# Seed products, clamps and K's skip term computed by GpSimd, x's first two splits in another order, and the last bank copied by ScalarE alone

## The chip, the cores and the metric

The kernel runs on one core of a Trainium2 chip. The metric is the device time of one execution in microseconds (us). Engines are named as the profile has them: PE is TensorE's matmul, PEld its weight load, DVE is VectorE, ACT is ScalarE, POOL is GpSimd, SP is SyncE, which here only issues DMAs.

## The reference

Two independent heads are computed and concatenated along the last axis. All inputs are fp32.

```python
# head A: FNet mixing, x is [1, 2048, 512]
a = jnp.einsum("bsd,ed->bse", x, dft_hid_re)
b = jnp.einsum("bsd,ed->bse", x, dft_hid_im)
y = jnp.einsum("ts,bse->bte", dft_seq_re, a) - jnp.einsum("ts,bse->bte", dft_seq_im, b)
...
# head B: S4D convolution, 512 channels, 128 states, length 2048
P = jnp.exp((A * dt[:, None])[:, :, None] * pos[None, None, :])
K = 2.0 * jnp.einsum("dn,dnl->dl", C, P).real
y = jnp.fft.irfft(jnp.fft.rfft(u_t, L2) * jnp.fft.rfft(K, L2)[None], L2)[:, :, :L]
y = y.transpose(0, 2, 1) + u * D_skip
```

## The kernel before, in words

**Head A** (class `Fnet`) is two stages of matmuls in split precision. Every fp32 operand is split into a high part, rounded to the type that PE multiplies fast, and a low part, the remainder; one product is then three matmuls of 128x128 by 128x512 (L371): high by high, high by low, low by high. `split` (L222) writes the high part on ScalarE (L226) and the low part on VectorE (L230). Stage "s" multiplies x, kept in SBUF as 16 tiles, with 8 blocks of the sequence matrices; stage "p" multiplies the transformed weights with the results. There are 128 streamed tiles in the first stage and 32 in the second, and the 28 of the first that `SOFTS` lists are split by DMA: POOL issues a load of the tile (L320), ScalarE writes its negative (L323), and POOL issues a second load that adds the source (L325). The four split tiles in flight come free when PE has used them. `evacuate` (L381) copies a finished bank on ScalarE (L396) and stores it; the very last bank is copied in halves, the right one by VectorE (L389) and the left one by ScalarE (L391), with one DMA each from SP and ScalarE.

**Head B** (class `Ssm`) builds the kernel K from two tables of complex powers per channel. The 512 channels go in 16 chunks of 32. For each chunk `seed_args` (L644) makes the arguments of the seeds on ScalarE, takes the phase's distance from its nearest whole number on VectorE (L662), clamps it to plus or minus a half (L664, the clamp, 352 elements a partition), and takes absolute value, exponential and sines on ScalarE (L666 to L674). `seeds` (L678) multiplies cosine and sine with the decay (L683, the product, 704 elements a partition, written with a stride of two) and ScalarE copies the result with either sign (L688). `tables1` and `tables2` double the tables with products and sums on VectorE (L613, L622, L636, L642) and squares on ScalarE (L629). `taps` multiplies the tables on PE (L809), ScalarE copies the taps `ks` to SBUF (L819), and `stage1_k` (L827) adds the skip term to one position (L832, 16 elements a partition) and runs the first half of K's transform on PE (L858). The spectra of u and K are then formed, multiplied (L1021 to L1057) and transformed back (L1064, L1136, L1158), through DRAM.

**What sets the order.** The program holds generators that yield the engine they want and a cost; `Plan` runs them against estimated clocks and thereby writes one fixed order for each engine, each of which runs it in order. A `yield "dve", ...` decides when the instruction behind it is emitted, whichever engine that instruction is for. So PE's order is fixed too: an L809 or L1064 that waits for VectorE holds up the L371 matmuls behind it.

Of the kernel before, what the change touches and what calls it, by code (L numbers as in the profile page):

```python
# [8 lines left out]
F32 = mybir.dt.float32  # L9
F32R = mybir.dt.float32r  # L10
I32 = mybir.dt.int32
AF = mybir.ActivationFunctionType
OP = mybir.AluOpType
# [3 lines left out]
SEQ, DM, NS = 2048, 512, 128  # L17
# [170 lines left out]
def act(cols):  # L188
    return 0.09 + cols * 0.00085


def dve(cols, rate=1.0):
    return (66 + cols / rate) / 960
# [6 lines left out]
class Fnet:  # L200
# [4 lines left out]
    def __init__(self, tc, ctx, plan, x, wT, sT, out):  # L205
        self.tc, self.nc, self.plan = tc, tc.nc, plan
        self.xin, self.wT, self.sT, self.out = x, wT, sT, out
        self.psum = ctx.enter_context(tc.tile_pool(name="a_psum", bufs=4, space=PSUM))
        self.pool = ctx.enter_context(tc.tile_pool(name="a", bufs=1))
        self.acc, self.raws, self.ss, self.ys = Sem(4), Sem(RAWS), Sem(DEPTH), Sem(STAGED)  # L210
        dram = ctx.enter_context(tc.tile_pool(name="a_dram", bufs=1, space=DRAM))
        self.p = {(t, c, d): dram.tile([128, DM], F32, name=f"p{t}_{c}_{d}")
                  for t in range(4) for c in range(2) for d in range(4)}
        self.p_ev = {k: Event() for k in self.p}
        self.x, self.w = [None] * 16, [None] * 8
        self.x_ev, self.w_ev, self.x_free = ([Event() for _ in range(n)] for n in (16, 8, 16))
        self.groups = [("s", t, c) for t in range(4) for c in range(2)] + [("p", t, None) for t in range(4)]
        self.items = {g: [(*g, k) for k in range(16 if g[0] == "s" else 8)] for g in self.groups}
        self.split_ahead, self.x0_ev, self.hi_ev = 0, Event(), Event()
        self.m, self.m_ev = {}, {i: Event() for g in self.groups for i in self.items[g]}  # L220

    def split(self, hi, lo, src):  # L222
        def urgency():
            return 3 if self.split_ahead >= AHEAD else 0
        yield "act", act(512), urgency
        self.nc.scalar.activation(hi, src, AF.Copy)  # L226
        if self.hi_ev.time is None:
            self.plan.set(self.hi_ev)
        yield "dve", dve(512), urgency
        self.nc.vector.tensor_tensor(lo, src, hi.bitcast(F32), op=OP.subtract)  # L230

    def start(self, buffers):
# [40 lines left out]
    def load_x1(self, b, raw, n):  # L273
        cols = slice(0 if n else 128, DM)
        yield "dma", load(256)
        self.nc.sync.dma_start(raw[:, cols], self.xin[n, :, cols])
        if n:
            self.x[n] = self.still(n)
        else:
            yield self.hi_ev  # L280
        yield from self.split(*(a[:, cols] for a in self.x[n]), raw[:, cols])
        self.plan.set(self.x_ev[n])
        self.x_left -= 1
        if not self.x_left:
            self.plan.put(b.uks)
# [95 lines left out]
    def evacuate(self, g, d, ps):  # L381
        yield self.ys
        y = self.pool.tile([128, DM], F32, name="y", bufs=STAGED)
        if g == self.groups[-1] and d == 3:
            out = self.out[128 * d:128 * d + 128, 512 * g[1]:512 * g[1] + 512]
            yield self.ys
            y2 = self.pool.tile([128, DM], F32, name="y", bufs=STAGED)
            yield "dve", dve(256)
            self.nc.vector.tensor_copy(y2[:, 256:], ps[:, 256:])  # L389
            yield "act", act(256)  # L390
            self.nc.scalar.activation(y[:, :256], ps[:, :256], AF.Copy)  # L391
            self.nc.sync.dma_start(out[:, 256:], y2[:, 256:])
            self.nc.scalar.dma_start(out[:, :256], y[:, :256])
            return
        yield "act", act(512)
        self.nc.scalar.activation(y, ps, AF.Copy, scale=-1.0 if g[2] == 1 else 1.0)  # L396
        self.plan.put(self.acc)
        if g != self.groups[-1]:
            yield "dma", load(256)
        kind, t, c = g  # L400
        if kind == "s":
            self.nc.sync.dma_start(self.p[t, c, d], y)
            self.plan.set(self.p_ev[t, c, d])
        else:
            self.nc.sync.dma_start(self.out[128 * d:128 * d + 128, 512 * t:512 * t + 512], y)
        self.plan.put(self.ys)
# [29 lines left out]
class Ssm:  # L436
# [207 lines left out]
    def seed_args(self, ck, box, ev):  # L644
# [9 lines left out]
        n = 11 * CHUNK  # L654
# [6 lines left out]
        yield "dve", dve(n)  # L661
        v.scalar_tensor_tensor(r, k, RND, r, op0=OP.subtract, op1=OP.subtract)  # L662
        yield "dve", dve(n, 2)
        v.tensor_scalar(r, r, 0.5, -0.5, op0=OP.min, op1=OP.max)  # L664
        yield "act", act(n)
        a.activation(k, r, AF.Abs)  # L666
        yield "act", act(n) + 1.3
# [10 lines left out]
    def seeds(self, ck, s):  # L678
# [1 line left out]
        yield self.css  # L680
        cs = self.tab.tile([128, 2, 11, CHUNK, 2], F32, name="cs", bufs=2)
        yield "dve", dve(22 * CHUNK)
        self.nc.vector.tensor_tensor(cs[:, :, :, :, 0], s[:, 1:3], s[:, 0:1].to_broadcast([128, 2, 11, CHUNK]),  # L683
                                     op=OP.mult)
        self.plan.put(self.res)
        for n, sign in enumerate((1.0, -1.0)):
# [140 lines left out]
    def stage1_k(self, ks, n, ev):  # L827
# [1 line left out]
        nc = self.nc  # L829
        yield ev  # L830
        yield "dve", dve(16)
        nc.vector.tensor_tensor(ks[:, 0], self.dskip[:, 16 * n:16 * n + 16], ks[:, 0], op=OP.add)  # L832
        yield self.const_ev
        got = yield from self.banks(2)
        xs = []
# [415 lines left out]
```

## Time and profile before

| | |
|---|---|
| median of 3 runs | 578.18 us (577.84 to 579.45) |
| profiled execution | 578.43 us, of which its span, first to last instruction, 576.6 us |
| granted TensorE clock | 0.998 |
| PE, PEld busy | 567.8 us (98%), 432.5 us (75%) |
| DVE, ACT, POOL busy | 523.1 us (91%), 371.1 us (64%), 40.2 us (7%) |
| chain that ended last | PE 53%, DVE 34%, issue 7% |

A row of a group reads: line, engine, operation, output from inputs, shapes, count, then busy us and the mean ns of one, then the idle time of the engine ahead of it and who ended it. A row of the timeline or of the chain begins with the start in us and the length in us. A row of a stage begins with the stretch and its length. A busy PE is the modelled length of its matmuls, which overlap, so a short wait can hide beneath one.

### The profile page before, as it was taken

How to read it: one execution, taken by the hardware profiler on the slowest of the kernel's cores; microseconds unless marked ns; L12 is line 12 of the kernel's file. 1: busy time of each engine (PE TensorE's matmuls, PEld its weight loads, DVE VectorE, ACT ScalarE, POOL GpSimd, SP SyncE). 2: the span in 40 equal slices, each digit the busy share in tenths (PEclk: the TensorE clock that was granted, in tenths of full speed). 3: DMA queues.
4: the chain of work that ended last, by engine and by line, in shares of the span. 5: the costliest groups of instructions: out<-in, count | busy, mean ns of one | idle time of the engine just before them, and what ended most of it. 6: DMA issues, size and time to landing. Idle time of an engine off the chain costs nothing.

```text
span 576.6 us, 15666 instructions
## 1 busy us (share of the span) xinstructions
PE 567.8 (98%) x6278; PEld 432.5 (75%) x6278; DVE 523.1 (91%) x928; ACT 371.1 (64%) x728; POOL 40.2 (7%) x60
## 2 busy tenths in 40 slices
PE   8999999999999999999999999999999999999997
PEld 6877777788777777778787777777787778776785
DVE  6999999999999999999999999999998999547732
ACT  4779766673777495858669576754588845355623
POOL 0000101000110000100100100001100000000000
PEclk9999999999999999999999999999999999999999
DMA  8999999997469767867796888559998996599994
GB/s 250 326 386 251 285 282 278 278 281 185 123 160 231 196 175 235 202 165 217 194 251 197 220 202 252 142 155 259 288 295 227 237 311 207 129 278 265 256 254 147
DMA packets 147976, 133.70 MB, mean 232 GB/s; under 512 B 47296, under 2 KB 107328, under 8 KB 147648
## 3 DMA queue, kind: packets, MB, share of 16 engines
q1 hardware_dynamic: 138976, 115.54, 66.7%
q0 software_dynamic: 8064, 14.68, 13.1%
q10 hardware_dynamic: 864, 2.49, 1.9%
q8 instruction: 49, 0.80, 0.6%
q14 instruction: 23, 0.19, 0.1%
HBM read 89.95 MB, written 42.73 MB: 230 GB/s over the span
## 4 chain that ended last, share of the span: by engine, by line
PE 53%; DVE 34%; issue 7%; DMA 3%; ACT 3%; SPq 0%; DVEq 0%; ACTq 0%
PE acc L371 41%; DVE prod L613 11%; DVE t L622 6%; DVE lo L230 5%; PE f L1037 4%; PE f L1064 3%; PE f L809 3%; DVE t L642 2%; DMA out_yb<-zl 1%; DVE cs L683 1%; DVE z L1021 1%; DVE uk L1023 1%; PE f L858 1%; DMA zl<-zs 1%; DVE zl L925 1%
## 5 line engine op out<-in xcount | busy, mean ns | idle before, releaser
L371 PE MATMUL acc<-hi,x_hi 128*128 128x512 f32 x640 | 257.9, 403 | 0.5 <-ACT x_hi L226 0.4
L371 PE MATMUL acc<-lo,x_hi 128*128 128x512 f32 x640 | 250.1, 391 | 0.0
L371 PE MATMUL acc<-hi,x_lo 128*128 128x512 f32 x640 | 249.6, 390 | 0.0
L613 DVE TENSOR_TENSOR prod<-t,cs 128x1024 f32<-128x1024 f32 (+4 forms) x192 | 163.1, 868 | 1.7 <-ACT t L731 0.6
L371 PEld LDWEIGHTS acc<-hi,x_hi 128*128 128x128 f32 x640 | 120.0, 187 | 49.7 <-issue 23.8
L371 PEld LDWEIGHTS acc<-hi,x_lo 128*128 128x128 f32 x640 | 120.2, 188 | 26.5 <-DVE x_lo L230 0.5
L371 PEld LDWEIGHTS acc<-lo,x_hi 128*128 128x128 f32 x640 | 120.2, 188 | 23.3 <-DVE lo L230 0.4
L226 ACT ACTIVATE hi<-raw 128x512 fp32r<-128x512 f32 x132 | 82.6, 628 | 68.2 <-PE acc L371 53.2
L230 DVE TENSOR_TENSOR lo<-raw,hi 128x512 fp32r<-128x512 f32 x132 | 90.1, 685 | 23.8 <-ACT hi L226 23.1
L622 DVE TENSOR_TENSOR t<-prod 128x512 f32<-128x512 f32 (+4 forms) x192 | 94.1, 511 | 1.0
L629 ACT ACTIVATE square<-t 128x256 f32<-128x256 f32 (+1 forms) x64 | 36.7, 573 | 29.3 <-DVE t L622 26.8
L325 POOL DMA_DIRECT2D lo<-in_sT x28 | 24.3, 867 | 214.1 <-DVE t L622 40.0
L1016 ACT ACTIVATE uk<-f 128x1024 f32<-128x1024 f32 x32 | 31.1, 1017 | 10.8 <-PE f L1037 7.8
L809 PEld LDWEIGHTS f<-t,t 128*32 128x32 f32 x2048 | 29.5, 110 | 7.4 <-issue 5.2
L396 ACT ACTIVATE y<-acc 128x512 f32<-128x512 f32 x47 | 27.8, 595 | 10.5 <-PE acc L371 10.3
L809 PE MATMUL f<-t,t 128*32 128x64 f32 x2048 | 32.4, 220 | 1.3 <-issue 0.8
L320 POOL DMA_DIRECT2D hi<-in_sT x28 | 16.1, 575 | 189.2 <-PE acc L371 148.6
L1079 ACT ACTIVATE z<-f 128x512 f32<-128x512 f32 x32 | 17.8, 592 | 13.1 <-PE f L1064 12.0
L1021 DVE TENSOR_TENSOR z<-uk 128x512 f32<-128x512 f32 x32 | 21.9, 684 | 4.4 <-ACT uk L1016 2.9
L642 DVE TENSOR_TENSOR t<-square 128x128 f32<-128x128 f32 (+1 forms) x64 | 24.7, 386 | 0.0
L1037 PE MATMUL f<-xt,w 64*32 64x256 f32 x768 | 23.5, 379 | 0.0
L1023 DVE TENSOR_TENSOR uk<-uk 128x512 f32<-128x512 f32 x32 | 22.1, 691 | 0.9
(101 smaller groups left out, 502.9 us busy)
## 6 DMA issues: line engine op xcount, KB each, us to landing
raw<-in_sT SPq DMA_DIRECT2D x99, 256.0 KB, 5.2
p<-y SPq DMA_DIRECT2D x32, 256.0 KB, 3.5
xk<-xk_sb SPq DMA_DIRECT2D x32, 256.0 KB, 5.2
zs<-z SPq DMA_DIRECT2D x32, 256.0 KB, 3.9
raw<-p SPq DMA_DIRECT2D x32, 256.0 KB, 4.3
hi<-in_sT POOLq DMA_DIRECT2D x28, 256.0 KB, 4.6
lo<-in_sT POOLq DMA_DIRECT2D x28, 256.0 KB, 4.7
xt<-xu SPq DMA_DIRECT2D x24, 256.0 KB, 4.4
```

The source lines that it names most:

```text
L226: self.nc.scalar.activation(hi, src, AF.Copy)
L230: self.nc.vector.tensor_tensor(lo, src, hi.bitcast(F32), op=OP.subtract)
L371: nc.tensor.matmul(acc[d], l[:, cols], r, start=k == 0 and n == 0, stop=k == len(items) - 1 and n == 2)
L396: self.nc.scalar.activation(y, ps, AF.Copy, scale=-1.0 if g[2] == 1 else 1.0)
L613: self.nc.vector.tensor_tensor(p.rearrange("p k d c m -> p k (d c) m"), src.rearrange("p d c l -> p (d c) l")[:, None, :, rows].to_broadca ...
L622: self.nc.vector.tensor_tensor(dst[:, :, :, rows], p[:, 0], p[:, 1, :, ::-1], op=OP.add)
L629: self.nc.scalar.activation(sq, t[:, :, :, m // 2:m], AF.Square)
L642: self.nc.vector.tensor_tensor(t[:, :, 0, m:2 * m:2], box[0][:, :, 0], box[0][:, :, 1], op=OP.subtract)
L809: nc.tensor.matmul(ps[32 * j:32 * j + 32, i], t1[:, d, c], t2[:, d, c], start=c == 0, stop=c == 1, tile_position=(0, 32 * j))
L1016: a.activation(uk[:, r].rearrange("p g c n d -> p g (c n d)"), p, AF.Copy)
L1023: v.tensor_tensor(t[:, r], t[:, r], u[:, r, :, ::-1], op=OP.mult)
L1037: nc.tensor.matmul(got[r][1][32 * xx:32 * xx + 32, g, 256 * c:256 * c + 256], self.w2[rows, 2 * q + r, xx, 32 * c:32 * c + 32], xt[rows].r ...
```

## The change

Five edits. `split` takes the tiles of x's items 0 and 1 in the order in which its two steps come to run (`first`, `turns`), so that the rest of tile 0 is split ahead of tile 1 on ScalarE and on VectorE. The last bank is copied whole by ScalarE, and both DMAs read that copy. The clamp, the product and the skip term are instructions of GpSimd; the lines that yield a slot of VectorE for them stay as they were.

```diff
+        self.first, self.turns = {}, {"hi": [0, 1], "lo": [0, 1]}
...
-    def split(self, hi, lo, src):
+    def split(self, *tiles, n=None):
...
         yield "act", act(512), urgency
+        hi, _, src = tiles if n is None or n > 1 else self.first[self.turns["hi"].pop(0)]
         self.nc.scalar.activation(hi, src, AF.Copy)
...
         yield "dve", dve(512), urgency
+        hi, lo, src = tiles if n is None or n > 1 else self.first[self.turns["lo"].pop(0)]
         self.nc.vector.tensor_tensor(lo, src, hi.bitcast(F32), op=OP.subtract)
...
-        else:
+        tiles = (*(a[:, cols] for a in self.x[n]), raw[:, cols])
+        if n < 2:
+            self.first[n] = tiles
+        if not n:
             yield self.hi_ev
-        yield from self.split(*(a[:, cols] for a in self.x[n]), raw[:, cols])
+        yield from self.split(*tiles, n=n)
...
-            yield self.ys
-            y2 = self.pool.tile([128, DM], F32, name="y", bufs=STAGED)
-            yield "dve", dve(256)
-            self.nc.vector.tensor_copy(y2[:, 256:], ps[:, 256:])
-            yield "act", act(256)
-            self.nc.scalar.activation(y[:, :256], ps[:, :256], AF.Copy)
-            self.nc.sync.dma_start(out[:, 256:], y2[:, 256:])
+            yield "act", act(512)
+            self.nc.scalar.activation(y, ps, AF.Copy)
+            self.nc.sync.dma_start(out[:, 256:], y[:, 256:])
             self.nc.scalar.dma_start(out[:, :256], y[:, :256])
...
-        v.tensor_scalar(r, r, 0.5, -0.5, op0=OP.min, op1=OP.max)
+        self.nc.gpsimd.tensor_scalar(r, r, 0.5, -0.5, op0=OP.min, op1=OP.max)
...
-        self.nc.vector.tensor_tensor(cs[:, :, :, :, 0], s[:, 1:3], s[:, 0:1].to_broadcast([128, 2, 11, CHUNK]),
+        self.nc.gpsimd.tensor_tensor(cs[:, :, :, :, 0], s[:, 1:3], s[:, 0:1].to_broadcast([128, 2, 11, CHUNK]),
...
-        nc.vector.tensor_tensor(ks[:, 0], self.dskip[:, 16 * n:16 * n + 16], ks[:, 0], op=OP.add)
+        nc.gpsimd.tensor_tensor(ks[:, 0], self.dskip[:, 16 * n:16 * n + 16], ks[:, 0], op=OP.add)
```

Line numbers move by 3 to 7: L226, L230 and L371 become L229, L234 and L378, L664, L683 and L832 become L667, L686 and L835, and POOL's DMAs L320 and L325 become L327 and L332.

The first place is ScalarE at the start of the program, where `x_hi_140` is the rest of x's tile 0 and `x_hi_150` is tile 1. Before:

```order
L335 DMA raw<-in_sT 128x512
L226 ACT_TABLE_LOAD
L226 ACTIVATE hi<-raw 128x512
L226 ACTIVATE x_hi_150<-uk 128x512
L226 ACTIVATE x_hi_140<-uk 128x384
L226 ACTIVATE hi<-raw 128x512
```

And with the change:

```order
L342 DMA raw<-in_sT 128x512
L229 ACT_TABLE_LOAD
L229 ACTIVATE hi<-raw 128x512
L229 ACTIVATE x_hi_140<-uk 128x384
L229 ACTIVATE x_hi_150<-uk 128x512
L229 ACTIVATE hi<-raw 128x512
```

The two splits of x have changed places, and nothing else here; VectorE's low parts of the two tiles change places in the same way.

The second place is VectorE near the end of the fourth chunk's first table, `t_1803`, where the second skip term (`ks`) and the sixth chunk's product (`cs<-seed`) stood; `prod` and `prod_2062` are products for the tables, `lo` is the low part of a streamed tile. Before:

```order
L613 TENSOR_TENSOR prod<-t_1803,cs 128x1024
L230 TENSOR_TENSOR lo<-raw,hi 128x512
L622 TENSOR_TENSOR t_1803<-prod 128x32x16
L230 TENSOR_TENSOR lo<-raw,hi 128x512
L832 TENSOR_TENSOR ks<-dskip,ks 128x16
L683 TENSOR_TENSOR cs<-seed 128x704
L613 TENSOR_TENSOR prod_2062<-t_124,cs 128x128
L613 TENSOR_TENSOR prod<-t_1803,cs 128x1024
```

And with the change:

```order
L616 TENSOR_TENSOR prod<-t_1803,cs 128x1024
L234 TENSOR_TENSOR lo<-raw,hi 128x512
L625 TENSOR_TENSOR t_1803<-prod 128x32x16
L234 TENSOR_TENSOR lo<-raw,hi 128x512
L616 TENSOR_TENSOR prod_2062<-t_124,cs 128x128
L616 TENSOR_TENSOR prod<-t_1803,cs 128x1024
```

The skip term and the product are gone from VectorE, and what stood behind them follows at once; all else on VectorE keeps its order, and PE's order is the same from end to end.

The third place is POOL at about the same point; `hi` and `lo` are the tiles that POOL loads, and `seed_1821`, `ks_1476` and `cs_2051` belong to the sixth clamp, the second skip term and the sixth product. Before, POOL's rows there are DMAs alone:

```order
L325 DMA lo_1748<-in_sT 128x512
L320 DMA hi_1856<-in_sT 128x512
L325 DMA lo_1857<-in_sT 128x512
L320 DMA hi_2045<-in_sT 128x512
L325 DMA lo_2046<-in_sT 128x512
L320 DMA hi_2194<-in_sT 128x512
```

And with the change:

```order
L332 DMA lo_1748<-in_sT 128x512
L327 DMA hi_1856<-in_sT 128x512
L667 TENSOR_SCALAR seed_1821<-seed_1821 128x352
L332 DMA lo_1857<-in_sT 128x512
L835 TENSOR_TENSOR ks_1476<-dskip_112,ks_1476 128x16
L686 TENSOR_TENSOR cs_2051<-seed_1821 128x704
L327 DMA hi_2045<-in_sT 128x512
L332 DMA lo_2046<-in_sT 128x512
```

POOL's clamps, skip terms and products stand between the two loads of one tile or between two tiles, each behind whatever DMA comes ahead of it. One more row comes first of all on POOL, `L667 ISA`, ahead of the first clamp.

## The prediction

> **What bounds the kernel now.** I read the busy shares first, then the engines by stage, then the chain of waits, and last the rows of the moved instructions. The first line of the page has two full engines:
>
> ```profile
> PE 567.8 (98%) x6278; PEld 432.5 (75%) x6278; DVE 523.1 (91%) x928; ACT 371.1 (64%) x728; POOL 40.2 (7%) x60
> ```
>
> The busy time by stage (length, then PE, PEld, DVE, ACT, POOL) says where each of the two has room:
>
> ```profile
> 0.00:14.40 14.40, 12.28 (x44) 8.75 (x44) 10.02 (x25) 6.91 (x11) 0.20 (x4) 1.00 0.80 250
> 41.00:210.00 169.00, 167.51 (x1572) 128.55 (x1570) 167.34 (x298) 115.34 (x235) 17.77 (x25) 1.00 0.83 233
> 248.00:330.00 82.00, 81.95 (x1069) 64.05 (x1067) 81.17 (x143) 56.85 (x118) 7.95 (x12) 1.00 0.78 209
> 330.00:457.00 127.00, 125.91 (x1555) 95.86 (x1554) 123.84 (x224) 90.95 (x182) 10.52 (x15) 1.00 0.83 226
> 562.00:576.60 14.60, 10.61 (x164) 7.86 (x162) 4.18 (x7) 4.35 (x8) 0.00 (x0) 0.93 0.46 145
> ```
>
> PE idles 2.1 us in the first stage and 4.0 in the last. In the three stages between that are shown it idles 1.49 + 0.05 + 1.09 = 2.6 us. DVE has little more room: 1.66 us from 41 to 210, 0.83 from 248 to 330, and 3.16 from 330 to 457. The chain of waits, in order of time, tells which of the two leads:
>
> ```profile
> 41.20 0.69 DVE z L927
> ...
> 210.00 1.20 PE f L1064 x32
> ...
> 247.89 0.18 DVE lo L230
> ...
> 330.32 1.12 PE f L858 x32
> ```
>
> It runs mainly along DVE from 41 to 210 and from 248 to 330, and along PE from 210 to 248 and from 330 on. In the two DVE stretches a microsecond more on DVE is about a microsecond more at the end, since PE takes its work in a fixed order and its work is not shortened. A microsecond less on DVE gives something only while PE has a stall left to lose.
>
> **The DVE work that goes.** These three groups leave DVE (busy us and mean ns behind the first bar):
>
> ```profile
> L683 DVE TENSOR_TENSOR cs<-seed 128x704 f32<-128x704 f32 x16 | 14.2, 885 | 0.0
> L664 DVE TENSOR_SCALAR seed<-seed 128x352 f32<-128x352 f32 x16 | 5.3, 334 | 0.0
> L832 DVE TENSOR_TENSOR ks<-dskip,ks 128x16 f32<-128x16 f32 x8 | 1.3, 168 | 0.1
> ```
>
> Neighbours on DVE overlap a little, so the chain has what one really occupies:
>
> ```profile
> 59.04 0.25 DVE seed L664
> ...
> 77.92 0.80 DVE cs L683
> ```
>
> That is 0.80 us for a product and 0.25 for a clamp (a skip term is no more than the 0.17 of its row, and I leave it out). In the two DVE stretches of the chain lie so many (count, first and last start; products and clamps in 41 to 210, then in 248 to 330):
>
> ```profile
> L683 DVE TENSOR_TENSOR cs<-seed x6: 880/883/886, 54.6 to 185.9; 128x704 f32<-128x704 f32 x6
> L664 DVE TENSOR_SCALAR seed<-seed x7: 332/334/336, 43.9 to 205.9; 128x352 f32<-128x352 f32 x7
> ```
> ```profile
> L683 DVE TENSOR_TENSOR cs<-seed x3: 883/884/884, 270.7 to 318.7; 128x704 f32<-128x704 f32 x3
> L664 DVE TENSOR_SCALAR seed<-seed x3: 331/332/334, 261.6 to 310.1; 128x352 f32<-128x352 f32 x3
> ```
>
> So 9 products and 10 clamps count: 9 x 0.80 + 10 x 0.25 = 9.7 us of DVE time off the stretches that lead. Those elsewhere lie beside PE work that leads, and I cost them at nothing either way: after 330 DVE's 3.16 us of idle time is their cover.
>
> **What the same work costs on GpSimd.** No row has POOL computing; its rows are DMA issues and four memsets. The nearest rows are DVE's own (0.885 and 0.334 us) and ScalarE's:
>
> ```profile
> L1016 ACT ACTIVATE uk<-f 128x1024 f32<-128x1024 f32 x32 | 31.1, 1017 | 10.8 <-PE f L1037 7.8
> L1079 ACT ACTIVATE z<-f 128x512 f32<-128x512 f32 x32 | 17.8, 592 | 13.1 <-PE f L1064 12.0
> L666 ACT ACTIVATE seed<-seed 128x352 f32<-128x352 f32 x16 | 8.0, 497 | 10.8 <-DVE seed L664 10.7
> ```
>
> Below, DVE's own 0.885 and 0.334; above, the two inputs of a product read one after the other at DVE's price, 2 x 0.885 = 1.77, and 2 x 0.334 = 0.67 for a clamp. Between them lies ScalarE's rate: (1017 - 592) / 512 = 0.83 ns an element, so 2 x 704 elements read in turn are 0.592 + (1408 - 512) x 0.00083 = 1.34 us, and a clamp is 0.50 as in L666. I take 1.34 and 0.50, as the middle of either pair (estimates).
>
> **What DVE does meanwhile.** No row shows POOL reading tiles beside DVE, so this is bounded too: DVE goes on (POOL's time costs it nothing) or stands still for all of it. I take the second. Almost every DVE group in those stretches (L613, L622, L230, L642) reads two SBUF operands, as the products on GpSimd would, and I see nothing that serves both at once without cost; that is a choice, not a reading. The Trainium skill speaks for it: SBUF — State Buffer, "Who interferes with whom", says that a DVE instruction with two SBUF inputs contends with a GpSimd instruction that reads SBUF, and that the second to issue waits for the whole of the first; no run here shows it yet. The skill's GPSIMD Engine Reference, "Elementwise — side-by-side cycle accounting", has about 2.6 cycles an element for two inputs, which at its 1.2 GHz would be 1.53 us for a product, an estimate; with 0.50 for a clamp the sum below would have 9.1 instead of 7.4.
>
> With DVE standing still the net is +1.34 - 0.80 = +0.54 for a product and +0.50 - 0.25 = +0.25 for a clamp: 9 x 0.54 + 10 x 0.25 = **+7.4 us**. DVE's idle 1.66 + 0.83 us in the two stretches can lie beneath some of it; I take off 1.0.
>
> **The waits.** ScalarE's absolute value (L666) waits for the clamp and its copies (L688) for the product, as before. Behind them in ScalarE's order stand the splits (L226) for PE. POOL starts a clamp as soon as L662 is done, and need not pass the DVE instructions that stood between; a product waits on POOL for the DMAs ahead of it. The worst place (POOL, then ScalarE):
>
> ```profile
> 376.16 0.86 POOL L325 DMA_DIRECT2D lo<-in_sT  x1 [6.19 <-DVE t L622]
> ```
> ```profile
> 377.17 0.98 ACT L688 ACTIVATE cs<-cs 128x352 f32<-128x352 f32 x2
> ```
>
> There the DMA ends at 377.02 and the product at 377.02 + 1.34 = 378.36, so L688 is 1.2 us late, in the stretch where PE leads. I cost the waits at nothing: ScalarE is 64% busy. The price if that cover is gone is 1.2 us a place. The skip term is waited for by PE itself (L858), 0.6 us in one place; on POOL it can be 0.1 to 0.5 longer or as much earlier, and I take zero. DMAs queued behind POOL's new work are issued up to 1.84 us later; they had waited for buffers anyway. A new ISA row stands ahead of POOL's first clamp; its cover is the 24 us until the first clamp's input is there:
>
> ```profile
> 24.36 0.52 DVE L662 SCALAR_TENSOR_TENSOR seed<-seed 128x352 f32<-128x352 f32 x1
> ```
>
> **The start.** ScalarE now converts the rest of x's first tile before the second tile, and DVE likewise:
>
> ```profile
> 5.13 1.04 ACT L226 ACTIVATE x_hi<-uk 128x512 fp32r<-128x512 f32 x2 [0.57 <-DMA uk<-in_x]
> ```
> ```profile
> 5.34 0.50 PE L371 MATMUL acc<-lo,x_hi 128*128 128x512 f32 x1
> 6.23 0.51 PE L371 MATMUL acc<-hi,x_hi 128*128 128x512 f32 x1 [0.39 <-ACT x_hi L226]
> ...
> 7.35 0.40 PE L371 MATMUL acc<-hi,x_hi 128*128 128x512 f32 x1
> 7.58 0.39 PE L371 MATMUL acc<-lo,x_hi 128*128 128x512 f32 x1
> ```
>
> Fed matmuls start 0.23 us apart (7.35 to 7.58). From 5.34 to 7.35 are four steps in 2.01 us, which fed are 0.92: at most 1.1 us goes. But DVE leads from 41 us on and has no less to do before, so part of the head start is waited away: between 0 and 1.1, I take 0.5.
>
> **The end.** The last bank was copied by DVE and then by ScalarE, and the last DMA left at 573.57:
>
> ```profile
> 572.65 0.42 DVE L389 COPY y<-acc 128x256 f32<-128x256 f32 x1 [6.79 <-DMA out_yb<-zl]
> ...
> 573.57 0.36 ACTq L393 DMA_DIRECT2D out_ya<-y  x1
> ```
>
> Now one copy of 512 columns at 0.59 (as L1079) from 572.65 ends at 573.24, and both DMAs leave about 573.28: 0.3 us sooner.
>
> **The sum.** The profiled execution took 578.43 us, of which its span is 576.6; the median of the runs is 578.18, so I take 0.25 off. 578.43 + 7.4 - 1.0 - 0.5 - 0.3 - 0.25 = **583.8 us**. Its own range has the cheapest POOL with DVE standing, 9 x 0.085 + 10 x 0.084 - 1.8 = about -0.2, hence 578.0, and the dearest, 9 x 0.97 + 10 x 0.42 = 12.9 without idle time taken off, hence 578.18 + 12.9 - 0.3 = 590.8.
>
> **The rivals.** First, and on the other side: **DVE goes on beside POOL**. Then 9.7 us leave the leading stretches, and PE's stalls are the limit. They are the 2.6 us above, and what the modelled ends hide; the longest wait of the weight loads for DVE in 41 to 330 is
>
> ```profile
> PEld f L1064 <- DVE uk L1057: 1.4, 3, 0.6
> ```
>
> so 1.4 us in three waits. Both together are 4.0 us, and other weight loads that waited for DVE or ScalarE, once each, can add a little; I take 5 us of stalls as gone, and 1.0 at the start since DVE no longer leads: 578.18 - 5 - 1.0 - 0.3 = **571.9 us**. It decides where POOL's reads cost DVE less than the 1.05 us that a product and a clamp leave free. For it speaks that the 132 rows of one DVE form differ by 0.02 us at most, though POOL issued 56 DMAs in the same time:
>
> ```profile
> L230 DVE TENSOR_TENSOR lo<-raw,hi x132: 674/684/694, 4.6 to 559.8; 128x512 fp32r<-128x512 f32 x132
> ```
>
> Against it, that a DMA issue from POOL reads a tensor in HBM and no tile, so it is weak evidence for an instruction that reads tiles.
>
> Second: **the two cancel**, POOL nearly as quick as DVE, or DVE half stopped: 9.7 us off and as much on, and the start and end gain 0.8: **577.4 us**.
>
> Third: **the queue on POOL decides**. Were each clamp and product late by the 1.2 us of the worst place, and ScalarE passed on half of it at the 10 clamps and 9 products that count, it would be 19 x 0.6 = 11.4 us: 578.18 + 11.4 - 0.8 = **588.8**. Against it: at 376.16 alone the DMA ahead of a product outlasts the turn that the product had on DVE.
>
> **Chances.** DVE stands still, 583.8: 0.57. DVE goes on: 0.26. Cancel: 0.12. Queue: 0.05. A change within 0.3% (1.7 us) is about what a measurement of this kernel cannot tell from none. Faster is 0.26, the same 0.12, slower 0.57 + 0.05 = 0.62. The range takes in the first rival, since 0.26 is more than may be left out: 571.5 to 590.5; the likeliest case alone is 578.0 to 590.8.
>
> **What would show it.** If right: DVE rows of one form with a tail of long ones, each beside a clamp (L667 in the changed file) or product (L686) on POOL; DVE busy rises though it has 41 fewer instructions; PE waits on DVE t and uk grow between 41 and 330; the first matmuls of L371 (L378 in the changed file) come closer; the last DMA leaves 0.3 us sooner after PE's end. If DVE's rows keep their lengths, my choice on DVE was wrong and PE's stalls shrink instead. If ScalarE's absolute values and copies (L669 and L691 there) wait for POOL far longer than they did for DVE, it was the queue.

## The result

The changed kernel took **598.69 us** (median of six runs, 595.46 to 601.69) beside 578.03 us for the kernel before on the same chip (577.82 to 579.99). The ratio is 1.034, with a 95% interval of 1.031 to 1.037: 20 us slower. The prediction had the right sign and was 15 us short; its range ended at 590.5. The medians in this document are over all runs of a kernel, and the ratios leave out one slow run each of *start_end* (625.43 us), *first_dve* (603.21) and *plan* (630.53), without which the medians are 578.50, 595.70 and 622.79.

The profiled execution took 595.49 us, next to the quickest of the six. Its busy line:

```profile
PE 572.3 (96%) x6278; PEld 432.7 (73%) x6278; DVE 533.3 (90%) x887; ACT 370.7 (62%) x728; POOL 101.1 (17%) x100
```

VectorE has 41 instructions fewer and is busy 10.2 us longer (523.1 before). The products and clamps that left had occupied 16 x 0.80 + 16 x 0.25 = 16.8 us there, so what stayed grew by some 27 us. The stages (length, then PE, PEld, DVE, ACT, POOL):

```profile
0.00:14.40 14.40, 12.56 (x47) 9.77 (x48) 9.81 (x25) 6.97 (x11) 0.20 (x4) 1.00 0.81 249
41.00:210.00 169.00, 163.02 (x1547) 124.42 (x1546) 163.43 (x272) 107.41 (x222) 42.84 (x38) 0.99 0.81 226
248.00:330.00 82.00, 79.56 (x936) 61.26 (x934) 79.94 (x133) 56.80 (x119) 21.02 (x19) 1.00 0.74 199
330.00:457.00 127.00, 122.77 (x1657) 92.11 (x1656) 123.54 (x204) 81.95 (x166) 21.89 (x25) 1.00 0.80 220
```

The first stage gained 0.3 us of PE time (12.28 before). PE's idle time from 41 to 210 went from 1.49 to 5.98 us, from 248 to 330 from 0.05 to 2.44, and from 330 to 457 from 1.09 to 4.23. DVE's went up too, in the first of these from 1.66 to 5.57 us. That is a first sign that longer DVE rows are not all: it waits more, too.

The moved instructions on GpSimd (min/median/max in ns, first and last start in us):

```profile
L686 POOL TENSOR_TENSOR cs<-seed x16: 1696/2096/4496, 30.3 to 470.0; 128x704 f32<-128x704 f32 x16
```
```profile
L667 POOL TENSOR_SCALAR seed<-seed x16: 471/776/2988, 25.1 to 462.1; 128x352 f32<-128x352 f32 x16
```
```profile
L835 POOL TENSOR_TENSOR ks<-dskip,ks x8: 223/386/732, 118.4 to 507.8; 128x16 f32<-128x16 f32 x8
```

One size of product takes between 1.70 and 4.50 us, one size of clamp between 0.47 and 2.99. Nothing about the instruction differs, so something holds it up. And on VectorE the form whose 132 rows lay between 674 and 694 ns before:

```profile
L234 DVE TENSOR_TENSOR lo<-raw,hi x132: 675/684/2504, 4.7 to 576.5; 128x512 fp32r<-128x512 f32 x132
```

The median is the old one; a few rows are very long. Who waits for GpSimd now:

```profile
ACT seed L669 <- POOL seed L667: 16.8, 11, 4.5
ACT cs L691 <- POOL cs L686: 16.6, 10, 3.7
ACT seed L659 <- POOL cs L686: 6.2, 2, 4.3
```
```profile
PE f L861 <- POOL ks L835: 2.9, 1, 2.9
```

ScalarE waits 39.6 us at these three lines (us, times, longest), where it waited 10.7 + 7.5 + 4.2 = 22.4 us for VectorE before.

One place shows both directions at once. GpSimd, then VectorE, then ScalarE, then TensorE (start, length, row):

```profile
111.19 4.50 POOL L686 TENSOR_TENSOR cs<-seed 128x704 f32<-128x704 f32 x1 [1.39 <-DVE prod L616]
...
118.41 0.73 POOL L835 TENSOR_TENSOR ks<-dskip,ks 128x16 f32<-128x16 f32 x1 [2.18 <-ACT ks L822]
```
```profile
111.89 0.69 DVE L234 TENSOR_TENSOR lo<-raw,hi 128x512 fp32r<-128x512 f32 x1
112.49 0.69 DVE L616 TENSOR_TENSOR prod<-t,cs 128x512 f32<-128x512 f32 x1
113.09 0.69 DVE L234 TENSOR_TENSOR lo<-raw,hi 128x512 fp32r<-128x512 f32 x1
113.69 0.42 DVE L625 TENSOR_TENSOR t<-prod 128x256 f32<-128x256 f32 x1
114.15 2.62 DVE L616 TENSOR_TENSOR prod<-t,cs 128x1024 f32<-128x1024 f32 x1
```
```profile
115.72 0.26 ACT L659 ACTIVATE seed<-par 128x64 f32<-128x64 f32 x1 [4.29 <-POOL cs L686]
...
117.74 0.58 ACT L822 ACTIVATE ks<-f 128x512 f32<-128x512 f32 x1
```
```profile
119.19 0.69 PE L861 MATMUL f<-ks,f1k 32*64 32x256 f32 x16 [2.87 <-POOL ks L835]
```

Read it in order. While GpSimd's product is "running", VectorE goes on at full speed: 111.89, 112.49, 113.09, 113.69, each begun about 0.09 us before the one ahead has ended. The row at 113.69 ends at 114.11 and the next begins at 114.15: for the first time a gap, 0.04 us. That next row takes 2.62 us in place of 1.22, and the product ends at 115.69, 1.54 us after it began. So GpSimd stood for 2.93 us and worked for about 1.57, and VectorE stood for 1.40 of these. Then the price of the delay: ScalarE's next seed (L659) needs the one seed buffer that the product still reads and waits 4.29 us; behind it in ScalarE's order stands the copy of the taps (L822), behind that the skip term, and TensorE waits 2.87 us.

I went through the GpSimd instructions above 2.5 us of the changed kernel and of the two kernels *clamps* and *products* below, 12 products and 3 clamps: every one has such a gap on VectorE (34 to 49 ns) inside it, every product ends 1.56 to 1.58 us after the gap opened, and every clamp 0.29 to 0.34 us after. The gap is not GpSimd's doing: the kernel before has it too, between the same two instructions and with no work on GpSimd (112.08 + 0.41 = 112.49, and the next begins at 112.52):

```profile
112.08 0.41 DVE L622 TENSOR_TENSOR t<-prod 128x256 f32<-128x256 f32 x1
112.52 1.23 DVE L613 TENSOR_TENSOR prod<-t,cs 128x1024 f32<-128x1024 f32 x1
```

A gap is where the long waits end, but GpSimd does not always need one. Many of the shorter products and clamps get in at the first boundary between two VectorE instructions that they meet, though the second begins before the first has ended. I took the 45 products and clamps of the same three kernels that began while VectorE ran, with no gap at the next boundary and no row from PSUM on either side of it (those with `f` as an input). Where VectorE's last gap lay at most 3.1 us back, all 18 got in at that boundary; where it lay 4.9 us back or more, none of 17 did; between the two, 7 of 10. It is a tendency and not a rule: in a second execution of the changed kernel the clamp at 59.12 us got in at its first boundary 6.7 us behind the last gap. Why a longer run of VectorE shuts GpSimd out is not shown.

### The profile page after: what moved, and what is told of

Same layout as the page of the kernel before. It is cut to its first block, busy times and chain, and to the rows that moved or that the text cites. A ratio compares the mean times of both kernels' runs of the same rounds, so it can differ in the third digit from the quotient of the medians.

```text
span 593.6 us, 15690 instructions
## 1 busy us (share of the span) xinstructions
PE 572.3 (96%) x6278; PEld 432.7 (73%) x6278; DVE 533.3 (90%) x887; ACT 370.7 (62%) x728; POOL 101.1 (17%) x100
## 4 chain that ended last, share of the span: by engine, by line
PE 40%; DVE 32%; ACT 8%; DMA 8%; issue 7%; SPq 2%; POOL 2%; DVEq 0%; POOLq 0%; ACTq 0%
PE acc L378 31%; DVE prod L616 10%; DVE t L625 6%; DVE lo L234 5%; PE f L1040 3%; DMA raw<-in_sT 2%; PE f L812 2%; DVE z L1024 2%; PE f L1067 2%; DMA uk<-in_x 2%; DVE t L645 2%; DVE uk L1026 2%; PE f L916 2%; DMA xt<-xu 1%; DVE xk_sb L848 1%
## 5 line engine op out<-in xcount | busy, mean ns | idle before, releaser
L378 PE MATMUL acc<-hi,x_hi 128*128 128x512 f32 x640 | 259.4, 405 | 2.7 <-ACT y L399 2.4
L378 PE MATMUL acc<-lo,x_hi 128*128 128x512 f32 x640 | 250.8, 392 | 0.0
L378 PE MATMUL acc<-hi,x_lo 128*128 128x512 f32 x640 | 249.9, 390 | 0.0
L616 DVE TENSOR_TENSOR prod<-t,cs 128x1024 f32<-128x1024 f32 (+4 forms) x192 | 167.7, 891 | 2.6 <-ACT t L754 0.8
L378 PEld LDWEIGHTS acc<-hi,x_hi 128*128 128x128 f32 x640 | 120.5, 188 | 54.2 <-issue 23.0
L378 PEld LDWEIGHTS acc<-hi,x_lo 128*128 128x128 f32 x640 | 120.7, 189 | 26.1
L378 PEld LDWEIGHTS acc<-lo,x_hi 128*128 128x128 f32 x640 | 120.7, 189 | 23.2 <-DVE lo L234 0.6
L234 DVE TENSOR_TENSOR lo<-raw,hi 128x512 fp32r<-128x512 f32 x132 | 97.4, 740 | 27.3 <-ACT hi L229 27.3
L229 ACT ACTIVATE hi<-raw 128x512 fp32r<-128x512 f32 x132 | 82.6, 628 | 60.8 <-PE acc L378 49.2
L625 DVE TENSOR_TENSOR t<-prod 128x512 f32<-128x512 f32 (+4 forms) x192 | 100.2, 543 | 1.1
L332 POOL DMA_DIRECT2D lo<-in_sT x28 | 24.8, 886 | 162.8 <-ACT lo L330 67.8
L686 POOL TENSOR_TENSOR cs<-seed 128x704 f32<-128x704 f32 x16 | 41.7, 2607 | 46.1 <-ACT seed L677 29.2
L399 ACT ACTIVATE y<-acc 128x512 f32<-128x512 f32 x47 | 27.8, 594 | 9.5 <-PE acc L378 9.5
L327 POOL DMA_DIRECT2D hi<-in_sT x28 | 16.7, 598 | 75.5 <-PE acc L378 45.8
L667 POOL TENSOR_SCALAR seed<-seed 128x352 f32<-128x352 f32 x16 | 16.3, 1016 | 72.8 <-DVE seed L665 71.1
L1024 DVE TENSOR_TENSOR z<-uk 128x512 f32<-128x512 f32 x32 | 24.7, 771 | 4.4 <-ACT uk L1019 2.9
L645 DVE TENSOR_TENSOR t<-square 128x128 f32<-128x128 f32 (+1 forms) x64 | 26.5, 413 | 1.9 <-ACT square L632 1.9
```

The source lines that it names most:

```text
L378: nc.tensor.matmul(acc[d], l[:, cols], r, start=k == 0 and n == 0, stop=k == len(items) - 1 and n == 2)
L616: self.nc.vector.tensor_tensor(p.rearrange("p k d c m -> p k (d c) m"), src.rearrange("p d c l -> p (d c) l")[:, None, :, rows].to_broadca ...
L625: self.nc.vector.tensor_tensor(dst[:, :, :, rows], p[:, 0], p[:, 1, :, ::-1], op=OP.add)
L645: self.nc.vector.tensor_tensor(t[:, :, 0, m:2 * m:2], box[0][:, :, 0], box[0][:, :, 1], op=OP.subtract)
L686: self.nc.gpsimd.tensor_tensor(cs[:, :, :, :, 0], s[:, 1:3], s[:, 0:1].to_broadcast([128, 2, 11, CHUNK]), op=OP.mult)
L1024: v.tensor_tensor(P[0][:, r], t[:, r], u[:, r], op=OP.mult)
```

## The experiments

Theory S: the loss is VectorE standing while GpSimd reads SBUF. Theory W: the loss is that GpSimd's result comes late, because a long run of VectorE without a gap keeps GpSimd out, and ScalarE, in order, passes the delay on. All but *gap3*, *plan*, *first_dve* and the repeats are built on *start_end*, which is the change without GpSimd's part.

### The parts alone

**start_end**: the diff without its GpSimd lines.

```
-        self.nc.gpsimd.tensor_scalar(r, r, 0.5, ...)      # all three lines back on nc.vector
+        v.tensor_scalar(r, r, 0.5, ...)
```

> The start and the end of the change alone (order of x's first two splits, last copy on ScalarE); clamps, products and skip terms are on VectorE as before. Both theories say the same here, since neither speaks of it: the start gives 0.85 us at matmul milestones of the changed kernel and the last DMA 0.3 us, so 576.9 us where before is 578.0 (ratio 0.998). If it is 580 or more, the loss of the change begins in the start, and both theories are short of a cause.

Measured 578.58 us, ratio 0.9999 (0.9988 to 1.0011). No gain. TensorE's block at 28 us, which began 0.85 us sooner in the changed kernel, begins 0.03 us later here, because TensorE took its first matmuls more slowly (rows in the part on why the prediction was wrong). The last DMA leaves at 572.96 us instead of 573.57, but the span is 576.6 us as before: from that DMA to the end it is 3.6 us in place of 3.1, and why is not shown. Both theories start from 578.6 us.

**clamps**, **products**, **skips**: *start_end* with one of the three lines on GpSimd.

```
-        self.nc.vector.tensor_tensor(cs[:, :, :, :, 0], ...)      # products; the others likewise
+        self.nc.gpsimd.tensor_tensor(cs[:, :, :, :, 0], ...)
```

> start_end with the 16 clamps on GpSimd and nothing else there. Theory S (VectorE stands while GpSimd reads SBUF, and that is the loss): VectorE loses about 0.55 us in a clamp of 0.6 to 0.8 us and is freed of 0.25 us, 0.3 us x 14 = +4 us over start_end, 581 us. Theory W (ScalarE, in order, waits for a result that comes later, and its next work is late for TensorE): a clamp comes some 0.5 us later than VectorE's, in a row of steps with 0.7 us of wait on ScalarE already, so most of 16 x 0.5 = up to +6 us, 583 us, with the loss seen as idle time of VectorE and not as longer rows.

Measured 582.43 us, ratio 1.0065 (1.0045 to 1.0084): 3.9 us over *start_end*. VectorE's busy time:

```profile
PE 571.3 (98%) x6278; PEld 434.8 (75%) x6278; DVE 522.8 (90%) x911; ACT 371.3 (64%) x728; POOL 61.8 (11%) x76
```

*start_end* has 522.9 there. What the clamps took from VectorE they gave back, so in sum none of the 3.9 us is theory S. The rows of GpSimd and the worst of them:

```profile
L667 POOL TENSOR_SCALAR seed<-seed x16: 508/780/7329, 25.7 to 451.9; 128x352 f32<-128x352 f32 x16
```
```profile
422.82 7.33 POOL L667 TENSOR_SCALAR seed<-seed 128x352 f32<-128x352 f32 x1 [2.81 <-DVE seed L665]
```

A clamp of 0.3 us of work took 7.33 us, with eleven VectorE instructions begun in it. TensorE's lag jumps by 4.0 us behind it (table below; this execution, 583.91 us, was the slowest of the four). That is theory W.

> start_end with the 16 products on GpSimd and nothing else there. Theory S: 1.36 us lost per product less 0.80 us given back, x 14 = +8 us over start_end, 585 us. Theory W: the product comes 1.2 us later and sometimes 3 us later, ScalarE's copy behind it and all that is queued behind that is late: +12 us or more, 589 us.

Measured 593.31 us, ratio 1.0248 (1.0218 to 1.0279): 14.7 us over *start_end*. VectorE is busy 532.7 us, 9.8 more. Both theories have a share.

> start_end with the eight skip terms on GpSimd and nothing else there. Theory S: nothing (16 elements in a partition), 577 us. Theory W: TensorE waited 2.9 us for this line in the changed kernel, but most of that lay behind a late product; with the queue of GpSimd empty the skip term comes 0.2 to 0.5 us later, 8 x 0.3 = +2 us at most, 578 us.

Measured 578.88 us, ratio 1.0006 (0.9993 to 1.0018). The skip terms alone cost nothing that can be measured.

The three parts add up: 3.9 + 14.7 + 0.3 = 18.9 us, where the whole change is 20.1 above *start_end*. The lag of TensorE shows where each arises (start of a block of TensorE instructions of one line less the start of the same block in the kernel before, us; the heading is its start before):

| kernel | 47.4 | 134.2 | 186.0 | 248.9 | 326.0 | 429.6 | 464.9 | 567.1 |
|---|---|---|---|---|---|---|---|---|
| start_end | 0.04 | -0.34 | -0.31 | -0.31 | -0.26 | -0.10 | -0.10 | -0.32 |
| clamps | 0.35 | 0.96 | 2.54 | 2.35 | 2.46 | 1.45 | 5.47 | 5.22 |
| products | 0.09 | 3.93 | 6.64 | 6.96 | 9.13 | 12.65 | 12.72 | 12.96 |
| changed kernel | 2.73 | 5.30 | 7.68 | 8.52 | 11.77 | 15.62 | 16.98 | 16.71 |
| changed kernel again | -0.01 | 4.38 | 6.24 | 7.56 | 10.81 | 13.39 | 19.00 | 19.18 |

### VectorE held, with nobody waiting

**extra_product**

```
         self.nc.vector.tensor_tensor(cs[:, :, :, :, 0], ...)
...
+        g.tensor_copy(x[:, 0:1], cs[:, 0, 0, 0:1, 0])      # paces it
+        g.tensor_tensor(x, x, x, op=OP.mult)               # 704 elements, never read
```

> start_end (clamps, products and skip terms on VectorE) with 16 products more on GpSimd: behind each product of VectorE, GpSimd copies one element of it (which paces it) and multiplies a tile of 704 elements in a partition with itself; nobody reads that tile. Theory S (VectorE stands while GpSimd reads SBUF): the other rows of VectorE lose 1.4 us each time, as in products: 16 x 1.4 = 22 us more of VectorE's busy time (545 us), some 18 to 22 us in all, 597 to 601 us. Theory W (the loss is waiting for a late result): nobody waits here, so 579 to 581 us.

Measured 596.24 us, ratio 1.0293 (1.0257 to 1.0329): 17.7 us over *start_end*.

```profile
PE 571.4 (96%) x6278; PEld 433.4 (73%) x6278; DVE 539.5 (91%) x927; ACT 371.4 (63%) x728; POOL 97.2 (16%) x93
```

VectorE does exactly the work of *start_end* and is busy 16.6 us longer, 1.04 us for each extra product (I had expected 1.4; these products multiply a tile with itself and take 1.36 us at the least). The time follows that sum at about 1.07 to 1. Theory S holds, and this run gives its exchange rate.

**extra_memset**: the same with `g.memset(x, 1.0)` twice in the place of the multiplication.

> extra_product with two memsets of the same tile of 704 elements in the place of the multiplication: GpSimd writes and reads nothing from SBUF but the one element. Theory S with reading as the cause: VectorE's rows stay as they are but for the 16 single elements, 579 to 581 us. If any work of GpSimd makes VectorE stand: in proportion to GpSimd's busy time, 10 us and more, 590 us.

Measured 578.57 us, ratio 0.9999 (0.9979 to 1.0018). The split rows of VectorE, beside 22 us of GpSimd memsets:

```profile
L234 DVE TENSOR_TENSOR lo<-raw,hi x132: 673/685/695, 4.5 to 559.5; 128x512 fp32r<-128x512 f32 x132
```

As before the change. What holds VectorE is not that GpSimd works, but that it reads SBUF. The Trainium skill, SBUF — State Buffer, "Who interferes with whom", says so: a VectorE instruction with two SBUF inputs contends only with a GpSimd instruction that reads SBUF. These rows agree, and so does the stretch at 114.15 above.

The single element that paces the memsets shows the other direction with nothing else beside it:

```profile
454.21 11.72 POOL L691 COPY scr<-cs 128x1 f32<-128x1 f32 x1 [10.58 <-DVE cs L688]
465.99 0.69 POOL L692 MEMSET scr<- 128x704 f32 x1
```

A copy of one element took 11.72 us, and VectorE did 17 instructions in that time, none of them longer than usual. Here I see no gap at its end; it ends at the end of a VectorE row of 0.37 us. In *extra_product* such a copy took 15.90 us, the longest of all.

### The wait, with VectorE hardly held

**one_element**

```
         self.nc.vector.tensor_tensor(cs[:, :, :, :, 0], ...)
+        self.nc.gpsimd.tensor_scalar(cs[:, 0, 0, 0:1, 0], cs[:, 0, 0, 0:1, 0], 1.0, None, op0=OP.mult)
```

> start_end with one GpSimd instruction behind each product: it multiplies one element in a partition of the product by 1.0, in place, so that ScalarE's next step waits for GpSimd and VectorE is hardly held (16 x about 0.1 us). Theory W with its mechanism (GpSimd gets in only where VectorE's back-to-back instructions leave a gap: in products every product above 2.5 us ended 1.57 us behind a gap of 34 to 49 ns): the single element takes 1 to 3 us at the same seven or eight places, and the time goes up by 4 to 8 us, 583 to 587 us. Without that mechanism the element takes 0.1 to 0.3 us everywhere, and the hop of two semaphores costs 2 us at most, 579 to 581 us.

Measured 581.74 us, ratio 1.0047 (1.0030 to 1.0064): 3.2 us above before, somewhat less than the 4 to 8 of theory W and more than the hop alone was to cost. VectorE is busy 523.1 us, 0.2 more than in *start_end*. The rows:

```profile
L688 POOL TENSOR_SCALAR cs<-cs x16: 227/588/7409, 38.1 to 456.0; 128x1 f32<-128x1 f32 x16
```

One element, 0.23 to 7.41 us, and ScalarE waited 20.5 us for it in 11 places, where it had waited 7.5 us for VectorE's product before. So a late result alone, without a held VectorE, costs some 3 us. How much of that is GpSimd kept out and how much the longer way over a further engine, this run does not part.

### A gap made on purpose

**clamps_gap** and **gap3**: *clamps* and the whole change, with a memset of one element on VectorE behind its next instructions (two after a clamp; in *gap3* also three after a product).

```
...
+        def spaced(f):
+            def g(*args, **kw):
+                r = f(*args, **kw)
+                if self.gaps:
+                    self.gaps -= 1
+                    v.memset(self.scr, 0.0)
+                return r
+            return g
+        v.tensor_tensor, v.scalar_tensor_tensor = spaced(v.tensor_tensor), spaced(v.scalar_tensor_tensor)
...
+        self.gaps = 2          # behind the clamp
+        self.gaps = 3          # behind the product, gap3 alone
```

> clamps (582.4 us; VectorE's busy time the same as in start_end, one clamp of 7.33 us and one of 2.98 us) with a memset of one element on VectorE behind each of the next two VectorE instructions after a clamp is handed over. Mechanism of gaps: no clamp above 1.5 us, the two stretches (around 155 and 423 us) where clamps lost 1.6 and 4.0 us at TensorE keep nearly level, and with 32 x 0.06 = 2 us of memsets at most the time is 579 to 581 us. If the loss of clamps is only the longer hop between engines, 582 to 584 us.

Measured 579.72 us, ratio 1.0021 (1.0008 to 1.0033). 32 instructions were added to VectorE, the busiest engine but one, and the kernel became 2.7 us quicker than *clamps*. The clamps:

```profile
L679 POOL TENSOR_SCALAR seed<-seed x16: 507/780/1909, 24.3 to 446.7; 128x352 f32<-128x352 f32 x16
```

The longest left is one of 1.91 us, above the 1.5 that I expected. It is the clamp of 2.98 us in *clamps*, and it got in right behind a memset. The clamp of 7.33 us is gone too, and TensorE's lag at 464.9 us is 0.36 in place of 5.47, but there no memset helped: that clamp (421.12) got in at the first boundary that it met, 0.69 us after VectorE had stood idle for 0.05 us. The same clamp was let in or kept out in two executions of one program (below). So the 2.7 us are clear of the scatter of the runs, but how many of them are the memsets' own work is not shown.

> The whole change, with memsets of one element on VectorE: one behind each of the next two VectorE instructions after a clamp is handed to GpSimd, and one behind each of the next three after a product. A memset reads nothing, so it should let GpSimd in. Mechanism of gaps: no product above 2.6 us and no clamp above 1.0 us, ScalarE's waits for them halved, 590 to 594 us where the change alone is 598. If GpSimd's long times have another cause: 598 to 601 us (the memsets alone cost 55 x 0.06 = 3 us of VectorE).

Measured 592.88 us, ratio 1.0230 (1.0184 to 1.0275): 5.8 us less than the changed kernel, though VectorE is busy 534.6 us, 1.3 longer. VectorE did 80 memsets (I had reckoned with 55). The waits did not halve: ScalarE's at the three lines above fell from 39.6 to 35.5 us, the longest product is 3.76 us and the longest clamp 1.91. But where a memset stands, it opens the way. The product of 111 us again (all VectorE rows of this kernel bear L460, the helper's line; L463 is the memset):

```profile
111.25 3.55 POOL L699 TENSOR_TENSOR cs<-seed 128x704 f32<-128x704 f32 x1 [1.40 <-DVE prod L460]
```
```profile
112.56 0.68 DVE L460 TENSOR_TENSOR prod<-t,cs 128x512 f32<-128x512 f32 x1
113.17 2.19 DVE L460 TENSOR_TENSOR lo<-raw,hi 128x512 fp32r<-128x512 f32 x1
113.19 0.06 DVE L463 MEMSET scr<- 128x1 f32 x1
```

GpSimd's product ends at 114.80, 1.55 us after the memset, and 0.95 us shorter than the 4.50 above. The split that came next stands for it, 2.19 us in place of 0.68.

### What a microsecond of VectorE is worth, the other way

**no_clamp**

```
-        v.tensor_scalar(r, r, 0.5, -0.5, op0=OP.min, op1=OP.max)
```

> start_end with the 16 clamps left out (a part of the computation that this kernel does not do). It measures what a microsecond of VectorE is worth: 16 x 0.25 = 4 us less of VectorE's busy time, and nothing waits longer. If VectorE sets the time in nearly all stretches, as the sum of the prediction had it, 575 us (3.3 to 4 us less). If VectorE's time is worth half, 577 us; if nothing, 578.6 us.

Measured 575.34 us, ratio 0.9940 (0.9921 to 0.9958): 3.2 us less for 3.8 us of VectorE (519.1 busy). So a microsecond of VectorE is worth about 0.85 us downward and 1.07 upward. This is the quickest of all kernels here, and it does less than the others; of those that do everything, none is quicker than the kernel before.

### Two that settled less

**first_dve** (and **first_dve_b** with **after_again** in the same rounds): the whole change, with the first chunk's clamp and product on VectorE.

```
-        self.nc.gpsimd.tensor_scalar(r, r, ...)
+        (self.nc.gpsimd if ck else v).tensor_scalar(r, r, ...)     # the product likewise
```

> The whole change but for the first of the 16 chunks, whose clamp and product stay on VectorE. In the changed kernel TensorE fell 3.6 us behind between 37 and 42 us, beside the first product. If that loss reaches the end, 598.7 - 3.6 = 595 us, and at 47 us TensorE is 0 to 0.4 us off the kernel before. If later waits of VectorE swallow it, as the early gain of start_end was swallowed, 598 us.

> first_dve once more (the whole change, the first chunk's clamp and product on VectorE), since its first trace can't be compared. If the 3.6 us that the changed kernel loses between 37 and 42 us reach the end: 3 to 4 us below after_again. If a later wait swallows them: within 1 us of it.

> The changed kernel unaltered, on the same chip and in the same rounds as first_dve_b, for the comparison of the two: 597 to 600 us, with TensorE 2 to 4 us late at 47 us.

Measured 596.48 us (ratio 1.026 to 1.032) and then 599.62 us (1.030 to 1.038) beside 597.85 for the changed kernel again (1.029 to 1.035). No gain from the first chunk. The table above says why: in its second profiled execution the changed kernel does not lose the 2.7 us at 47 us at all, and between 429.6 and 464.9 it loses 5.6 us where the first loses 1.4. The same clamp of the same program in the two:

```profile
436.46 1.31 POOL L667 TENSOR_SCALAR seed<-seed 128x352 f32<-128x352 f32 x1 [2.59 <-DVE seed L665]
```
```profile
435.10 7.33 POOL L667 TENSOR_SCALAR seed<-seed 128x352 f32<-128x352 f32 x1 [2.79 <-DVE seed L665]
```

In both, the clamp begins 0.25 us after the same VectorE row, L616, and meets its first boundary 0.97 us later:

```profile
436.21 1.22 DVE L616 TENSOR_TENSOR prod<-t,cs 128x1024 f32<-128x1024 f32 x1
437.34 0.97 DVE L234 TENSOR_TENSOR lo<-raw,hi 128x512 fp32r<-128x512 f32 x1
```
```profile
434.85 1.22 DVE L616 TENSOR_TENSOR prod<-t,cs 128x1024 f32<-128x1024 f32 x1
435.99 0.68 DVE L234 TENSOR_TENSOR lo<-raw,hi 128x512 fp32r<-128x512 f32 x1
```

In the first execution GpSimd gets in at that boundary, and the split behind it is the longer for it. In the second it passes ten boundaries and gets in at a gap. What differs is what VectorE had done before: in the first it had been idle for 0.23 us, 0.69 us ahead of the clamp; in the second it had run for 5.5 us without a gap. That goes with the wider scatter: 6.2 us between the changed kernel's quickest and slowest run, 2.2 for the kernel before.

**plan**: the planner is told that the moved instructions belong to GpSimd.

```
-        yield "dve", dve(n, 2)         # the clamp; product: "pool", 2.1; skip term: "pool", 0.4
+        yield "pool", 0.8
```

> The whole change, with the planner told of it: the 40 moved instructions take a slot of GpSimd of 0.8, 2.1 and 0.4 us in place of VectorE's slot, so the order on every engine is worked out anew. Theory S alone: VectorE is held by GpSimd as before, 596 to 600 us. Theory W: ScalarE's dependent steps are put later behind other work, so its waits for GpSimd fall from 39.6 us to less than half, and VectorE's extra idle time with them: 591 to 595 us. Below 590 us would say that the order was the main cause.

Measured 624.05 us, ratio 1.0760 (1.0716 to 1.0803). Both expectations failed. VectorE is busy 535.3 us, little more than in the changed kernel, but TensorE's lag grows from 10 us at 326 to 32 at 465, and ScalarE's wait for the clamp goes up to 23.6 us. The order is another one on every engine, so this run says only that a new order from these slots is no remedy; which of its moves costs the 25 us I did not take apart.

## Why the prediction was wrong

**VectorE stands while GpSimd reads.** Right, and the step that carried the sign. I took 1.34 us for a product and 0.50 for a clamp. Measured by VectorE's busy time over that of *start_end*, with what was given back added: 532.7 - 522.9 + 16 x 0.80 = 22.6 us in *products*, 1.41 each; 522.8 - 522.9 + 16 x 0.25 = 3.9 us in *clamps*, 0.24 each. Less the 0.80 and 0.25 given back, a clamp is free on VectorE, where I had put 0.25, and a product costs 0.61 net, near my 0.54.

**"Those elsewhere lie beside PE work that leads, and I cost them at nothing either way."** Wrong. I counted 9 products and 10 clamps out of 16 and 16. In *products* TensorE's lag still grows by 3.8 us after 326 us, where I had the 3.16 us of VectorE's idle time as cover; from 210 to 248 it grows by 0.7. All of them count: 16 x 0.61 = 9.8 us, and the busy lines of the whole change have 533.3 - 523.1 = 10.2. At the rate of *extra_product* that is 10.9 us in place of my 7.4 - 1.0.

**"I cost the waits at nothing: ScalarE is 64% busy."** This is the step that failed. 20.1 us over *start_end* less 10.9 leaves about 9 us. (The two profiled executions of the changed kernel, each with its own time and busy time, leave 6 us and 11 us, so the share of the waits is known only roughly.) That it is waiting, the parts say: *clamps* loses 3.9 us with no more VectorE time, *one_element* 3.2, and the kernels with memsets are quicker by 2.7 us (*clamps_gap*) and 5.8 (*gap3*). A mean of 64% says nothing of an engine that works in order: behind ScalarE's wait for one seed stood the copies and splits that TensorE needs. For copies of finished banks alone (L399) TensorE now waits 2.4 us in three places, where it did not wait before. I had the price of such a wait, 1.2 us a place, from GpSimd's own duration and the DMA ahead of it. I did not see that what I had quoted for VectorE works against GpSimd too, and that a VectorE which has run for some 5 us without a gap seldom lets GpSimd in between two of its instructions. The rows that should have told me were those of the stages: a VectorE that idles 1.66 us in 169 has few gaps.

**The skip term**, taken as zero: right by itself (*skips*). Its 2.87 us at 119 us are the product's delay passed on.

**The start and the end**, -0.5 and -0.3: nothing in *start_end*, within -0.7 and +0.6 us. In the first execution of the changed kernel the first matmuls do come closer, as I said:

```profile
5.33 0.39 PE L378 MATMUL acc<-hi,x_lo 128*128 128x512 f32 x1
5.56 0.43 PE L378 MATMUL acc<-lo,x_hi 128*128 128x512 f32 x1
5.83 0.40 PE L378 MATMUL acc<-hi,x_hi 128*128 128x512 f32 x1
6.06 0.39 PE L378 MATMUL acc<-lo,x_hi 128*128 128x512 f32 x1
```

TensorE is 0.85 us ahead at 28 us, and then it waits. In *start_end* they are fed as well, but come 0.43 us apart instead of 0.23 until 7.29 us, where the kernel before stands at 7.35:

```profile
5.16 0.63 PE L378 MATMUL acc<-hi,x_lo 128*128 128x512 f32 x1
5.58 0.63 PE L378 MATMUL acc<-lo,x_hi 128*128 128x512 f32 x1
...
7.29 0.48 PE L378 MATMUL acc<-hi,x_hi 128*128 128x512 f32 x1
```

The second execution of the changed kernel does the same. So the step from "fed" to "0.23 us apart" fails in some executions, though the granted clock is shown as 1.00 there; over the executions with this start TensorE is between 0.08 us behind and 0.86 ahead at 28 us. What decides it is not shown.

**The rivals.** "DVE goes on beside POOL" is excluded by *extra_product*, "cancel" holds for the clamps' VectorE time alone. "The queue on POOL decides" had the right engine waiting and the wrong reason: what held the six products above 2.5 us was VectorE, inside their own rows, while only four of the 16 began right behind a DMA.

**The signs that I named** came but for one, the wait of PE on `t`, of which PE's waits show none: long single rows of VectorE beside GpSimd's, its busy time up, more wait on `uk` (L1067 for L1057: 2.2 us in 4 waits), and ScalarE's waits for GpSimd, which I had named as the sign of the queue.

## What to carry to other kernels

Work moved from a nearly full VectorE to GpSimd costs VectorE the time in which GpSimd reads SBUF: for the products here more than they had taken on VectorE itself (1.41 us against 0.80), for the clamps about as much. The result can also come late, by as long as VectorE runs without a gap, and an in-order engine that waits for it hands the delay on to work that has nothing to do with it; so ask of a moved instruction who waits for it, before asking whether the old engine becomes free. An engine's mean share of busy time is no cover for a wait.

## What the runs showed of the hardware that I had not expected

- Behind a run of VectorE of some 5 us without a gap, a GpSimd instruction that reads SBUF mostly got in only at a gap of 34 to 49 ns between two VectorE instructions, or behind a memset of one element; one of a single element waited through 17 VectorE instructions (11.72 us). Early in such a run (up to 3.1 us) all 18 that I counted got in at the first boundary, with no gap. VectorE rows that read one input from PSUM were not held: beside the product at 79.16 us the two of L928 and L930 kept their 0.68 and 0.69 us. The Trainium skill, SBUF — State Buffer, "Who interferes with whom", says that the second waits for the whole of the first instruction; on VectorE's side the rows agree, on GpSimd's side the wait was many instructions long.
- GpSimd's own time with the way open was about 1.57 us for 704 elements of two inputs. The Trainium skill's GPSIMD Engine Reference, "Elementwise — side-by-side cycle accounting", with 2.6 cycles an element, gave the estimate of 1.53 us; my own from ScalarE's rate, 1.34, was too low.
- In the changed kernel TensorE idled 0.94 us at 38 us, and then its matmuls came 0.43 us apart instead of 0.23 for some 3 us (the granted clock of 25 to 41 us is 0.95):

```profile
38.46 1.11 PE L916 MATMUL f<-xt,f1u 32*64 32x512 f32 x8 [0.94 <-DVE zl L930]
...
40.10 0.63 PE L378 MATMUL acc<-lo,x_hi 128*128 128x512 f32 x1
40.52 0.63 PE L378 MATMUL acc<-hi,x_lo 128*128 128x512 f32 x1
40.95 0.63 PE L378 MATMUL acc<-hi,x_hi 128*128 128x512 f32 x1
```

That is about 1.2 us more than the idle time itself. After the longer idle time at 119.19 us (2.87) nothing of the kind is seen. But in *products*, behind 2.27 us of idle time at the same line, the matmuls from 117.97 to 120.96 come 0.43 us apart, with a granted clock of 0.50, and so do those from 454.82 to 457.80 in the changed kernel's second execution, behind 3.35 us. So a part of what the waits cost comes as slower matmuls behind them; what decides it stays open.
